# A long-convolution kernel: PSUM banks given out by the scheduler, three filter buffers, and float32r moved from two matmul groups to two others

## The chip, the cores and the metric

The kernel runs on one core of one Trainium2 chip. The metric is the device time of one execution in microseconds (us). Times of a kernel are medians over several executions. Engines are named as in the profile: PE is TensorE (matmuls), PEld its loading of weights, DVE is VectorE, ACT is ScalarE, POOL is GpSimd, SP is the engine that issues transfers. "L710" is line 710 of the kernel. The two versions have different line numbers for the same thing; where it matters, both are given.

## The reference

Four batches of 6272 positions and 256 channels go through a gated recurrence, a projection into three parts, a circular convolution along the positions (by Fourier transform), a product of three, and an output projection.

```python
# x, f_logit: (4, 6272, 256); lower_bound: (256,)
f = lower_bound + (1 - lower_bound) * sigmoid(f_logit)
h = 0
for t in range(6272):                      # the recurrence
    h = f[:, t] * h + (1 - f[:, t]) * x[:, t]
    hh[:, t] = h
x1, x2, x3 = split(hh @ w_proj, 3)         # (4, 6272, 256) each
X2 = rfft(x2, axis=1); H = rfft(filter_fft, axis=0)
y = x1 * irfft(X2 * H, axis=1) * x3
out = y @ w_out                            # float32
```

## The kernel before

The 6272 positions are 49 times 128, and the Fourier transform is made of two matmul stages. For each batch there are three stages that will be called P, U and O.

- **P**: projection to x2 and first transform.
- **U**: sixteen frequency units. Each makes the second transform (TensorE), the product with the filter's transform Hu (VectorE), and the first inverse transform (TensorE).
- **O**: thirteen groups of four residues. Each makes the second inverse transform (TensorE), the product with z = x1 times x3 (VectorE), and the output projection (TensorE).

The recurrence R of the next batch (transposes on TensorE, a scan on VectorE, x1 and x3 on TensorE) has no fixed place; it fills gaps. Before everything comes the preparation, which makes the filter's transform and writes it to DRAM, together with the first R.

No stage is ordered by hand. Every operation is declared with its cost, its reads and its writes. A greedy list scheduler then writes each engine's program: it repeatedly takes the operation that could start first by its estimate and, at equal times, the one with the longest tail behind it. PSUM banks are named in the declaration:

```python
def bank(*k):
    return [("b", i) for i in k]

# U: one pair of banks for the second transform, one for the inverse,
# except in the last batch, which has two of each
k = u % 2
xb, ib = (4 * k, 4 * k + 2) if b == B - 1 else (0, 2)
for i, (p0, p1, q0, ab) in enumerate(((0, TB, 0, 0), (0, Q, Q, 1), (Q, TB, 0, 1))):
    op({"SP": 0.5}, ... dma_start(Hu[p0:p1, k, ab], H[u][q0:q0 + p1 - p0]),
       r=[("H", u)], w=[("Hu", k, i)], kb=2 * (p1 - p0))
op({"PE": 0.5}, mm, r=[("E", u)], w=bank(xb, xb + 1))           # second transform
...
op({"DVE": 1.15}, prod, r=bank(xb + o) + [("Hu", k, i) ...])     # product, L626
...
op({"PE": 0.96}, inv, ..., w=bank(ib, ib + 1))                   # first inverse
```

The output stage writes y in f16 with m outside and the four residues i inside. The projection uses y as its stationary operand and w_out in two f16 halves, Woh + Wol:

```python
y = y[:, :, 0:rn * 128].rearrange("p a (m i) -> p a m i", i=rn)
nc.vector.tensor_tensor(y, PS[...], zr[:, :, :, r0:r0 + rn], op=AOP.mult)       # L672
for i in range(rn):
    for kh in range(2):
        for w in (Woh, Wol):
            nc.tensor.matmul(po[:, i, :], y[:, kh, :, i], w[:, kh, :], ...)     # L685
```

In R, the scan writes h in float32r, x1 and x3 are matmuls from it in float32r (L277), and GpSimd casts h to f16 (L269). In the preparation the filter is rotated by a matmul in plain float32. The copies that wrap h around (`wraps()`) are scheduled only after the preparation has been written out.

Of the kernel before, what the change touches and what calls it, by code (L numbers as in the profile page):

```python
# [21 lines left out]
S = 6272  # L22
# [28 lines left out]
class Plan:  # L51
# [5 lines left out]

    LAT = {"PE": 0.2, "ACT": 0.16, "DVE": 0.14, "POOL": 0.16, "SP": 0.0}
    OWN = {"PE": 0.0, "ACT": 0.1, "DVE": 0.08, "POOL": 0.1, "SP": 0.0}

    def __init__(self):
        self.ops, self.writer, self.readers = [], {}, {}
        self.free = {e: 0.0 for e in self.LAT}
        self.dma = 0.0
        self.table = None

    def op(self, cost, fn, r=(), w=(), kb=0.0, table=None):
# [4 lines left out]
        for t in w:  # L72
            if t in self.writer:
                preds.add(self.writer[t])
            preds.update(self.readers.get(t, ()))
        me = len(self.ops)
        self.ops.append(dict(cost=cost, fn=fn, preds=preds, kb=kb, table=table, end=None,
                             eng=None, succ=[]))
# [16 lines left out]

    def emit(self):
# [8 lines left out]
        while cand:  # L105
            best = None
            for e, f in self.free.items():
                pick = None
                for i in cand:
                    o = ops[i]  # L110
                    if e in o["cost"]:
                        at = max(f, self.ready(o, e))
                        if o["table"] and self.table and o["table"] != self.table:
                            at += 1.3
                        key = (at, -o["level"], i)
                        if pick is None or key < pick:
                            pick = key
                if pick is not None:
                    o = ops[pick[2]]
                    key = (pick[0] + (o["cost"][e] if len(o["cost"]) > 1 else 0.0) * 0.01,  # L120
                           pick[1], pick[2], e, pick[0])
                    if best is None or key < best:
                        best = key
            i, e, at = best[2:]
# [8 lines left out]
            o["fn"](e)  # L133
# [8 lines left out]
def kernel(  # L142
# [29 lines left out]
    W13 = konst.tile([128, 2, 512], F32R, name="W13")  # L172
    W2 = konst.tile([128, 2, 256], F16, name="W2")
    Woh = konst.tile([128, 2, 256], F16, name="Woh")
    Wol = konst.tile([128, 2, 256], F16, name="Wol")
# [10 lines left out]
    hs = konst.tile([128, 2, 2, CH], F32R, name="hs")  # L186
# [3 lines left out]
    H = [dram.tile([TB, 2, UE * 64], F16, name=f"H{u}") for u in range(NU)]  # L190
# [11 lines left out]

    def bank(*k):
        return [("b", i) for i in k]
# [23 lines left out]
    def hgrn(b):  # L228
        z = zt[b % 2]
        for c in range(NCHK):  # L230
# [14 lines left out]
            hk = c % 2  # L245
            for kh in range(2):
                cols = slice(kh * 128, kh * 128 + 128)
                sT, uT = PS[:, 6, 0:n], PS[:, 7, 0:n]

                def turn(e, dst, src, cols=cols, nb=nb):  # L250
                    for j in range(nb):
                        nc.tensor.transpose(dst[:, j * 128:(j + 1) * 128], src[:, j, cols],  # L252
                                            iden[:])
                op({"PE": 0.108 * nb}, lambda e, f=turn, d=sT, s=ft: f(e, d, s),
                   r=[("ft", k)], w=bank(6))
                op({"PE": 0.108 * nb}, lambda e, f=turn, d=uT, s=xt: f(e, d, s),
                   r=[("xt", k)], w=bank(7))
                j = count["f"] % 2
                count["f"] += 1
                fT, h = fTs[:, j, 0:n], hs[:, kh, hk, 0:n]  # L260
                op({"ACT": 0.13 + n / 1200.0}, lambda e, fT=fT, sT=sT, kh=kh:
                   nc.scalar.activation(fT, sT, AF.Identity, scale=nomc[:, kh:kh + 1],  # L262
                                        bias=1.0), r=bank(6), w=[("fT", j)])
                init = 0.0 if c == 0 else hs[:, kh, 1 - hk, CH - 1:CH].bitcast(F32)
                op({"DVE": 0.07 + 2.25 * n / 1000.0}, lambda e, h=h, fT=fT, uT=uT, init=init:
                   nc.vector.tensor_tensor_scan(h, fT, uT, init, op0=AOP.mult, op1=AOP.add),  # L266
                   r=bank(7) + [("fT", j), ("h", kh, 1 - hk)], w=[("h", kh, hk)])
                hn = HA[:, HB[kh] + t0:HB[kh] + t0 + n]
                op({"POOL": 0.1 + n / 1000.0}, lambda e, hn=hn, h=h: nc.gpsimd.tensor_copy(  # L269
                    hn, h.bitcast(F32)), r=[("h", kh, hk)], w=[("hn", kh, c)])  # L270
            for jb in range(2):
                for i in range(2):
                    js = slice(i * 256 + jb * 128, i * 256 + jb * 128 + 128)

                    def mm(e, i=i, js=js, hk=hk, n=n):
                        for kh in range(2):
                            nc.tensor.matmul(PS[:, 4 + i, 0:n], W13[:, kh, js],  # L277
                                             hs[:, kh, hk, 0:n], start=(kh == 0),
                                             stop=(kh == 1))
                    op({"PE": 2 * (0.06 + n / 2400.0)}, mm, r=[("h", 0, hk), ("h", 1, hk)],  # L280
                       w=bank(4 + i))
                j = count["s"] % 2
                count["s"] += 1
                xs = x1s[:, j, 0:n]
                op({"ACT": 0.06 + n / 1200.0}, lambda e, xs=xs, n=n: nc.scalar.activation(  # L285
                    xs, PS[:, 4, 0:n], AF.Copy, scale=ZS), r=bank(4), w=[("x1s", j)])
                op({"DVE": 0.07 + n / 960.0}, lambda e, zz=z[:, jb, t0:t0 + n], xs=xs, n=n:
                   nc.vector.tensor_tensor(zz, PS[:, 5, 0:n], xs, op=AOP.mult),  # L288
                   r=bank(5) + [("x1s", j)], w=[("z", b % 2, jb, c)])
# [12 lines left out]
    def prepare(tmp):  # L302
        dve, pool, act = nc.vector, nc.gpsimd, nc.scalar
        raws = [HA[:, S + 4096 * k:S + 4096 * (k + 1)].bitcast(F32)
                .rearrange("m (r d) -> m r d", d=D) for k in range(3)]
        hws = [HA[:, S + 12288 + 2048 * k:S + 12288 + 2048 * k + 1024]
               .rearrange("p (a n) -> p a n", a=2) for k in range(2)]
# [10 lines left out]
        def oms(e):  # L318
# [6 lines left out]
        wp = raws[0][:, 0:6].rearrange("p a d -> p (a d)").rearrange("p (k j) -> p k j", k=2)  # L325
        wo = raws[1][:, 0:2]
        op({"SP": 0.5}, lambda e: nc.sync.dma_start(
            wp, moe_w_proj.rearrange("(a p) j -> p a j", p=128)), w=E(0, 4096), kb=768)
        op({"SP": 0.5}, lambda e: nc.sync.dma_start(
            wo, moe_w_out.rearrange("(a p) j -> p a j", p=128)), w=E(4096, 8192), kb=256)  # L330
        for kh in range(2):
            small(lambda e, kh=kh: dve.tensor_scalar(
                wp[:, kh, :], in0=wp[:, kh, :], scalar1=omc[:, kh:kh + 1], scalar2=None,
                op0=AOP.mult), 768, r=["om"], w=E(0, 4096))
            for i, j0 in enumerate((0, 512)):
                small(lambda e, kh=kh, i=i, j0=j0: dve.tensor_copy(
                    W13[:, kh, i * 256:(i + 1) * 256], wp[:, kh, j0:j0 + 256]), 256,
                    r=E(0, 4096), w=["W13"])
            for p in range(2):
# [3 lines left out]
                    .rearrange("k (e g) -> k e g", e=2)), 256, r=E(0, 4096), w=["W2"])  # L343
        small(lambda e: dve.tensor_copy(Woh[:], wo[:]), 512, r=E(4096, 8192), w=["Wo"])
        small(lambda e: dve.tensor_tensor(Wol[:], wo[:], Woh[:], op=AOP.subtract), 512,
              r=E(4096, 8192), w=["Wo"])
# [105 lines left out]
        rot = tmp.tile([128, 256], F32, name="rot")  # L452
# [10 lines left out]
        small(gaps, 1920, r=["iden"], w=["f2e"], e="POOL")  # L463
        fv = f2[:, 0:NEP * PW].rearrange("m (g p c) -> m p g c", p=2, c=PW)
        ff = moe_filter_fft.rearrange("(a r) d -> a r d", r=Q)
        for g, r0 in enumerate(range(0, Q, 4)):
            rn = min(4, Q - r0)
            k = (g // 2 + 2) % 3
            raw, et = raws[k], E(4096 * k, 4096 * (k + 1))
# [291 lines left out]
```

## Time and profile before

| | before |
|---|---|
| time, median of 3 runs | 731.81 us (728.07 to 734.73) |
| preparation and first R, with most of a stop at its end | 131 us |
| P of the four batches | 32, 26, 23, 23 us |
| U of the four batches | 70, 76, 76, 54 us |
| O of the four batches | 59, 59, 58, 45 us |
| VectorE's product waiting for Hu | 37.0 us |
| TensorE's second transform waiting for that product | 30.3 us |

Two lines of the profile page of the kernel before give the totals: first the busy time of each engine with its share of the span and its number of instructions, then the clock granted to TensorE in 40 slices of the span, in tenths.

```profile
PE 617.1 (84%) x5262; PEld 471.1 (64%) x5262; DVE 513.9 (70%) x572; ACT 379.6 (52%) x485; POOL 203.2 (28%) x256
...
PEclk9999997699887999999778999999978999955599
```

No engine is busy throughout; in the second U, TensorE and VectorE are each busy for 62 of 76 us. The stage table, the waits and the end of the chain are shown in the prediction below.

### The profile page before, as it was taken

What the parts mean: (1) busy time and instruction counts of PE and PEld (TensorE: products, weight loads), DVE (VectorE), ACT (ScalarE), POOL (GpSimd) and SP (SyncE); (2) the same over time, 40 slices, a digit from 0 to 9 for tenths busy, and PEclk for the clock granted to TensorE, in tenths of its full rate; (3) what the DMA queues carried; (4) which work ended last, traced back from release to release, by engine and by line L of the source; (5) the groups of instructions that cost most, each with busy time, mean ns of one, the idle gap of its engine ahead of it and who ended that gap; (6) DMA issues with size and microseconds to landing.
All of it is one profiled execution on the core that took longest, in us unless ns stands there. A gap on an engine that the chain in (4) does not pass through costs nothing. (4 is left out here: it accounts for less than half of the span.)

```text
span 731.7 us, 13373 instructions
## 1 busy us (share of the span) xinstructions
PE 617.1 (84%) x5262; PEld 471.1 (64%) x5262; DVE 513.9 (70%) x572; ACT 379.6 (52%) x485; POOL 203.2 (28%) x256
## 2 busy tenths in 40 slices
PE   4889993588878999888888999978769999677896
PEld 3767772574546887864556887845448888444585
DVE  8987772389787666697877665898676666967542
ACT  4578882485433555774333556854424547422232
POOL 4335451223323332033223333033324310010000
PEclk9999997699887999999778999999978999955599
DMA  9755646336565757155465766155746732034144
GB/s 308 279 167 162 204 151 232 127 88 204 182 194 175 241 194 268 41 175 175 160 201 181 239 216 239 58 168 181 215 149 227 242 151 82 22 115 131 45 193 160
DMA packets 82161, 126.95 MB, mean 173 GB/s; under 512 B 5454, under 2 KB 56722, under 8 KB 81330
## 3 DMA queue, kind: packets, MB, share of 16 engines
q1 hardware_dynamic: 82098, 126.10, 52.8%
q8 instruction: 41, 0.67, 0.4%
q14 instruction: 22, 0.18, 0.1%
HBM read 84.54 MB, written 28.90 MB: 155 GB/s over the span
## 5 line engine op out<-in xcount | busy, mean ns | idle before, releaser
L626 DVE TENSOR_TENSOR PP<-PS,Hu 98x1008 f16<-98x1008 f32 x128 | 147.8, 1198 | 46.1 <-DMA Hu<-H 37.0
L277 PE MATMUL PS<-hs,W 128*128 128x512 f32 (+1 forms) x416 | 140.5, 432 | 16.3 <-ACT x1s L285 10.9
L243 POOL TENSOR_TENSOR XT<-XT,FL 128x1024 f32<-128x1024 f32 (+1 forms) x52 | 116.7, 2244 | 86.0 <-DMA XT<-in_x_dram 61.2
L209 ACT CAST X<-PS 128x784 f16<-128x784 f32 (+2 forms) x86 | 87.1, 1020 | 86.4 <-PE PS L637 71.7
L269 POOL CAST HA<-hs 128x512 f16<-128x512 f32 (+1 forms) x104 | 61.6, 593 | 245.3 <-DVE hs L266 236.1
L266 DVE TENSOR_TENSOR_SCAN hs<-fTs,hs,PS 128x512 fp32r<-128x512 f32 (+1 forms) x96 | 115.9, 1207 | 10.6 <-PE PS L252 8.9
L672 DVE TENSOR_TENSOR PP<-PS,z 128x1024 f16<-128x1024 f32 (+1 forms) x52 | 61.1, 1184 | 82.7 <-PE PS L663 76.8
L262 ACT ACTIVATE fTs<-PS,nomc 128x512 f32<-128x512 f32 (+1 forms) x104 | 69.1, 665 | 80.1 <-DVE hs L266 42.6
L637 PEld LDWEIGHTS <-PP 98*128 98x128 f16 x1024 | 64.3, 118 | 51.0 <-issue 34.2
L685 PE MATMUL PS<-Woh,PP 128*128 128x256 f16 x392 | 90.3, 278 | 3.4 <-DVE PP L672 3.0
L685 PEld LDWEIGHTS <-PP 128*128 128x128 f16 x784 | 82.6, 114 | 15.8 <-issue 7.6
L277 PEld LDWEIGHTS PS<-hs,W 128*128 128x128 f32 x416 | 66.8, 196 | 35.3 <-ACT x1s L285 15.4
L685 PE MATMUL PS<-Wol,PP 128*128 128x256 f16 x392 | 89.0, 275 | 0.0
L616 PE MATMUL PS<-HA,FT 64*128 64x512 f16 x256 | 59.5, 458 | 31.7 <-DVE PP L626 30.3
L637 PE MATMUL PS<-VA,PP 98*128 98x98 f16 x512 | 72.9, 244 | 15.2 <-DVE PP L626 11.7
L211 ACT ACTIVATE osb<-PS 128x1024 f32<-128x1024 f32 (+1 forms) x51 | 50.3, 986 | 66.3 <-PE PS L685 37.5
L241 ACT ACTIVATE FL<-FL 128x1024 f32<-128x1024 f32 (+1 forms) x52 | 52.4, 1008 | 61.5 <-DMA FL<-in_f_logit_dram 61.5
L288 DVE TENSOR_TENSOR z<-PS,x1s 128x512 f16<-128x512 f32 (+1 forms) x104 | 67.1, 645 | 15.6 <-PE PS L277 9.9
L252 PE MATMUL PS<-iden,FL 128*128 128x128 f32 x392 | 67.1, 295 | 12.8 <-ACT FL L241 10.8
L285 ACT ACTIVATE x1s<-PS 128x512 f32<-128x512 f32 (+1 forms) x104 | 59.3, 570 | 28.9 <-DVE z L288 15.8
L637 PE MATMUL PS<-VB,PP 98*128 98x98 f16 x512 | 73.5, 245 | 0.0
L252 PE MATMUL PS<-iden,XT 128*128 128x128 f32 x392 | 69.9, 304 | 3.4 <-DVE hs L266 3.4
(89 smaller groups left out, 711.3 us busy)
## 6 DMA issues: line engine op xcount, KB each, us to landing
FL<-in_f_logit_dram SPq DMA_DIRECT2D x48, 512.0 KB
XT<-in_x_dram SPq DMA_DIRECT2D x48, 512.0 KB
out_dram<-osb SPq DMA_DIRECT2D x48, 512.0 KB
Hu<-H SPq DMA_DIRECT2D x64, 196.0 KB
Hu<-H SPq DMA_DIRECT2D x128, 98.0 KB
HA<-in_moe_filter_fft_dram SPq DMA_DIRECT2D x6, 1024.0 KB
HA<-HA SPq DMA_DIRECT2D x16, 384.0 KB
H<-HA SPq DMA_DIRECT2D x16, 196.0 KB
```

The costliest lines, as they stand in the source:

```text
L209: nc.scalar.copy(dst, src)
L243: op({"POOL": 0.1 + 0.535 * nb}, lambda e, xt=xt, ft=ft: nc.gpsimd.tensor_tensor(xt, xt, ft, op=AOP.mult), r=[("ft", k)], w=[("xt", k)])
L252: nc.tensor.transpose(dst[:, j * 128:(j + 1) * 128], src[:, j, cols], iden[:])
L262: nc.scalar.activation(fT, sT, AF.Identity, scale=nomc[:, kh:kh + 1], bias=1.0), r=bank(6), w=[("fT", j)])
L266: nc.vector.tensor_tensor_scan(h, fT, uT, init, op0=AOP.mult, op1=AOP.add),
L269: op({"POOL": 0.1 + n / 1000.0}, lambda e, hn=hn, h=h: nc.gpsimd.tensor_copy(hn, h.bitcast(F32)), r=[("h", kh, hk)], w=[("hn", kh, c)])
L277: nc.tensor.matmul(PS[:, 4 + i, 0:n], W13[:, kh, js], hs[:, kh, hk, 0:n], start=(kh == 0), stop=(kh == 1))
L288: nc.vector.tensor_tensor(zz, PS[:, 5, 0:n], xs, op=AOP.mult),
L626: nc.vector.tensor_tensor(PP[:TB, k, o, :, :, 1:64], px.unsqueeze(1).broadcast_to([TB, 2, UE, 63]), hh[:, :, :, 1:64], op=AOP.mult)
L637: nc.tensor.matmul(PS[:, ib + o, pr * TB:(pr + 1) * TB], PP[:TB, k, o, n, 2 * pr:2 * pr + 2, :], v[:TB], start=(n == 0), stop=(n == 1))
L672: nc.vector.tensor_tensor(y, PS[:, cb:cb + 2, 0:rn * 128].rearrange("p a (m i) -> p a m i", i=rn), zr[:, :, :, r0:r0 + rn], op=AOP.mult),
L685: nc.tensor.matmul(po[:, i, :], y[:, kh, :, i], w[:, kh, :], start=(n == 0), stop=(n == 3))
```

## The change

The intent has five parts.

1. **Banks.** An operation says how many banks it takes (`take=2`), the scheduler gives it any free pair, and the readers (`src=`) give it back.
2. **x1 and x3** are computed in f16 from the f16 h, which the scan now writes itself. GpSimd's 104 casts go.
3. **Output projection** in float32r: one matmul instead of two f16 halves, with y and w_out in float32r.
4. **H in three buffers**: the second, swapped copy of each filter tile is written to DRAM once in the preparation, so that a unit needs one load of 392 KB instead of three, and Hu has three buffers instead of two.
5. **Filter rotation** in float32r after a cast, and the wraps in the first schedule.

```diff
+    def room(self, n):
+        best = None
+        for b in range(0, 8, n):
+            if None not in self.bank[b:b + n]:
+                key = (max(self.bank[b:b + n]), n == 1 and self.bank[b ^ 1] is not None, b)
+                if best is None or key < best:
+                    best = key
+        return best
 ...
-    W13 = konst.tile([128, 2, 512], F32R, name="W13")
+    W13 = konst.tile([128, 2, 512], F16, name="W13")
-    Woh = konst.tile([128, 2, 256], F16, name="Woh")
-    Wol = konst.tile([128, 2, 256], F16, name="Wol")
+    Wo = konst.tile([128, 2, 256], F32R, name="Wo")
 ...
-                                             hs[:, kh, hk, 0:n], start=(kh == 0),
+                                             HA[:, HB[kh] + t0:HB[kh] + t0 + n],
 ...
-            pb = 2 * (g % 2)
-            def rotate(e, r0=r0, rn=rn, raw=raw, pb=pb):
+            op({"POOL": 0.1 + 0.3 * rn, "ACT": 0.1 + 0.22 * rn, "DVE": 0.1 + 0.27 * rn},
+               lambda e, raw=raw, fr=fr, rn=rn: copy(e, fr[:, 0:rn], raw[:, 0:rn]),
+               r=et, w=[("af", g % 2)])
+            def rotate(e, pb, r0=r0, rn=rn, fr=fr):
 ...
-            op({"SP": 0.5}, lambda e, hw=hw, u=u: nc.sync.dma_start(H[u][:], hw[:TB]),
-               r=ht, w=[("H", u)], kb=200)
+            for i, (p0, p1, q0) in enumerate(((0, TB, 0), (0, Q, Q), (Q, TB, 0))):
+                op({"SP": 0.5}, lambda e, hw=hw, u=u, p0=p0, p1=p1, q0=q0, ab=min(i, 1):
+                   nc.sync.dma_start(H[u][p0:p1, ab], hw[q0:q0 + p1 - p0]),
+                   r=ht, w=[("H", u, i)], kb=2 * (p1 - p0))
 ...
-            xb, ib = (4 * k, 4 * k + 2) if b == B - 1 else (0, 2)
-            for i, (p0, p1, q0, ab) in enumerate(((0, TB, 0, 0), (0, Q, Q, 1), ...
+            h = (b * NU + u) % 3
+            op({"SP": 0.5}, lambda e, h=h, u=u: nc.sync.dma_start(Hu[:TB, h], H[u][:]),
+               r=[("H", u, i) for i in range(3)], w=[("Hu", h)], kb=400)
 ...
-            op({"PE": 0.5}, mm, r=[("E", u)], w=bank(xb, xb + 1))
+            f2 = op({"PE": 0.5}, mm, r=[("E", u)], take=2)
 ...
-            y = PP[:, yk // 2, yk % 2].rearrange("p a i k -> p a (i k)")
-            y = y[:, :, 0:rn * 128].rearrange("p a (m i) -> p a m i", i=rn)
+            y = ys[:, yk, :, 0:rn * 128].rearrange("p a (m i) -> p a m i", i=rn)
 ...
-                        for w in (Woh, Wol):
-                            nc.tensor.matmul(po[:, i, :], y[:, kh, :, i], w[:, kh, :],
-                                             start=(n == 0), stop=(n == 3))
+                        nc.tensor.matmul(po[:, i, :], y[:, kh, :, i], Wo[:, kh, :],
+                                         start=(kh == 0), stop=(kh == 1))
 ...
-        Hu = cv.tile([128, 2, 2, 2, UE * 64], F16, name="Hu")
+        Hu = cv.tile([128, 3, 2, 2, UE * 64], F16, name="Hu")
+        ys = cv.tile([128, 2, 2, 512], F32R, name="ys")
```

The diff gives y two buffers instead of four.

## The prediction

The sum in it came to 647 us:

- The float32r projection at 125 to 167 ns a matmul (49 to 65 us for 392; in the sum 14 us of the first O, and 1.0 to 1.4 us a group in the last) was an estimate from a rate that no trace shows. A straight line between the two float32r rows that the text names, 112 ns at 128 columns and 231 at 512, gives 152 ns for 256, inside that range; the 0.15 us for a matmul of the rotation, also an estimate, is near it.
- The 24 us of the first P is near the 26, 23 and 23 of the others before.

What the text calls half clock is shown: granted 0.50 from 659 to 687 us, and over the whole kernel before L637 starts every 81 ns where 0.50 was granted and every 43 where it was 1.0.

> **What bounds the kernel now.** I read four views: the page's totals, a table of busy time by stage, the waits, and the chain that ended last. The stages were found by where the groups of TensorE matmuls begin and end in the timeline. A batch has a projection and first transform (P, 23 to 26 us), sixteen frequency units (U) and the output stage (O). The recurrence of the *next* batch (R: transposes, scans, x1 and x3) runs under U and O. Filter preparation and the first R come before all.
>
> The table of stages (length, then busy us and count of PE, PEld, DVE, ACT, POOL, then granted clock, DMA share, GB/s): preparation, then U, O and P of the second batch, then U and O of the last.
> ```profile
> 0.00:131.00 131.00, 100.71 (x597) 77.35 (x597) 91.82 (x164) 84.87 (x119) 53.60 (x76) 0.96 0.67 218
> ...
> 292.00:318.00 26.00, 23.46 (x256) 21.82 (x254) 17.58 (x16) 20.14 (x21) 3.49 (x3) 0.93 0.23 80
> 318.00:394.00 76.00, 62.08 (x472) 40.02 (x471) 62.24 (x61) 33.09 (x46) 24.95 (x33) 0.81 0.56 177
> 394.00:453.00 59.00, 58.60 (x530) 48.04 (x527) 37.01 (x41) 31.16 (x44) 21.01 (x20) 0.98 0.71 237
> ...
> 633.00:687.00 54.00, 39.25 (x324) 22.19 (x323) 39.63 (x36) 13.02 (x17) 5.05 (x16) 0.58 0.35 105
> 687.00:731.70 44.70, 36.73 (x392) 32.72 (x392) 15.37 (x14) 12.67 (x13) 0.00 (x0) 0.92 0.37 145
> ```
> The reader is to see two limits in alternation. O is TensorE's: 58.6 of 59 us. U is VectorE's with holes: 62.2 of 76 us. In U of the last batch nothing else runs, and VectorE is still busy for only 39.6 of 54.
>
> The waits (who waited for whom, us, times, longest):
> ```profile
> DVE PP L626 <- DMA Hu<-H: 37.0, 26, 3.3
> ...
> PE PS L616 <- DVE PP L626: 30.3, 34, 4.1
> ...
> PE PS L550 <- DMA HA<-HA: 17.7, 2, 13.6
> ```
> The first two are the holes of U: VectorE's product waits for the filter tile Hu, and TensorE cannot write the next unit before VectorE has read the single pair of banks. The third is a 13.6 us stop before the first P, because the copies that wrap h around are issued only after the preparation is complete.
>
> The end of the last O, in the chain (start, us, what):
> ```profile
> 694.92 3.62 PE PS L685 x32
> 698.54 1.00 PE PS L663 x16
> 699.54 0.02 issue
> 699.56 1.23 DVE PP L672
> 700.80 0.05 issue
> 700.84 3.68 PE PS L685 x32
> ```
> Two groups take 5.9 us: 32 projection matmuls (3.68), 16 inverse ones, and VectorE in between, exposed.
>
> [...]L685 (256 columns) starts every 109 ns, L565 (128) every 56. [...]weights of L685 take 114 ns, those of float32r L277 take 196. [...]
>
> **The change part by part.**
>
> *Output projection.* Out: 784 f16 matmuls at 109 ns, 85.5 us. In: 392 float32r ones. No row has 128x256 float32r. L277 (512 columns, float32r) starts every 231 ns inside a run[...], and the first of a run costs 85 more (316); L496 (128 columns) every 112. [...] TensorE gets back 20 to 36 us, in O, where it is the bound: 5 to 9 us per batch.
>
> *x1 and x3 in f16.* 416 matmuls in pairs; a pair now takes 316 + 231 = 547 ns, in f16 about 2 x 216 + 60 = 490 or less. That is 12 to 20 us of TensorE, a third in O. GpSimd's 104 casts (61.6 us) go, off the path. The scan stays at 1.27 us.
>
> *Filter rotation.* The old form has 98 rows for 49 products (two passes), each starting 215 ns after the last: 21.1 us. The new: 49 x 0.15 = 7. It adds thirteen casts to float32r, by the order of instructions ten on ScalarE at about 1.0 us and three on GpSimd. TensorE gains 14, ScalarE loses 10. Moreover the wraps are in the first schedule, the filter tiles being laid out clear of them: most of the 17.7 us goes.
>
> *Filter tile.* One load of 392 KB into three buffers instead of three loads into two; the second copy is written once (3.1 MB more). It attacks the 37.0 us, all inside U.
>
> *Banks.* Any free pair instead of fixed ones: attacks the 30.3 us, and the 1.23 us per two groups of the last O.
>
> The order of instructions of the changed kernel shows something the diff does not: in the first U, VectorE has its 32 products without one scan between. All 26 scans of the second batch's R fall into the first O. In the second U there are ten scans, in the third three scans and fourteen x1x3 products.
>
> **Sum by stage**, from what each engine would need:
> - Preparation: VectorE 91.8 + 3 (three more evictions), ScalarE 84.9 + 7, TensorE down to about 80. Plus 10 us of start and some holes: 112 instead of 131.
> - First P: 24 instead of 32[...].
> - First U: 32 products x 1.17 = 37.5 and 1.8 for the edge; TensorE at half clock needs about 2.6 us per unit (1.04 for L616, 2 x 0.62 for L637, and gaps), 42. I take 44, was 70.
> - First O with all of R: TensorE 14 (inverse) + 14 (projection) + 21.4 (196 transposes x 109 ns) + 26 (x1, x3) = 75; VectorE 31.5 (scans) + 17 (x1x3) + 15.4 (products of O) + 4 = 68. Thirteen loads of 1 MB and 6.4 MB of output also want some 250 GB/s. I take 80, was 59.
> - Second and third batch: P 24 and 24 (were 26, 23). U: 37.5 + 1.8 + 13 of scans or x1x3 products = 53, I take 54 each (was 76). O: TensorE about 62 to 68 by the same addition; that addition gives 64 for the old O against 59 measured, so I scale it to 63 and 62 (59, 58).
> - Last: P 23. U 46 (VectorE 41 plus ramp; was 54). O: 13 groups at 2.5 us (TensorE 1.0 + 1.0 to 1.4, output through two buffers) plus ends, 37 (was 45).
>
> 112 + 24 + 44 + 80 + 24 + 54 + 63 + 24 + 54 + 62 + 23 + 46 + 37 = **647 us**, 11.6% less. By stage, U gives 78 us (two waits go, and R moves out), the preparation 19 and P 9; O takes 21 back, because R moves into it, though its own matmuls shrink.
>
> **Rivals.**
> (a) *Loads bound the first O.* x and f_logit keep two buffers, and one chunk's round is load, sigmoid (1.06), GpSimd product (2.37), transposes. At 5.5 to 6.5 us a chunk that is 70 to 85 us, as long as the stage. For it: loads already stop ScalarE for 61.5 us. If copies queue, this O takes 90 to 95 and the total is 660. Against: only 0.71 of the DMA engines' time was used at 237 GB/s.
> (b) *The clock takes it back.* [...]TensorE at half clock (42 us) bounds U. With transposes on top, U of the middle batches is 60: total 660.
> (c) *Projection in float32r is not cheaper*, its weights being loaded with a stride[...]. At 218 ns it gives back 9 us per batch: total about 675.
> (d) *The schedule fits better than I think.* VectorE needs about 515 us in all; at 85% busy (70% now) the time is 606.
>
> **Range.** Taking out two measured waits (67 us, near the bound in U) and 46 to 70 us of TensorE gives a clear gain; (a) to (c) together hardly undo it. I predict 647, 8 in 10 between 618 and 682. Faster by over 2%: 0.97; within 2%: 0.02; slower: 0.01.
>
> **What would show it.** Right: waits of L658 (the product) for Hu under 8 us in all; waits of L648 for it under 10; first P starting near 112 us with no multi-microsecond stop on a copy; the first and last U 42 to 46 us with VectorE over 85% busy; the float32r projection starting every 125 to 167 ns; GpSimd near 140 us busy; total VectorE unchanged near 515. Wrong: a first O over 90 us with waits on x or f_logit (rival a); U of the middle batches at 60 or more with a clock under 0.75 (b); the projection at 200 ns or more (c). The whole would be wrong if evictions to other types, or scans writing f16, were slower than their old rows.

## More of the kernel before

The granted clock is lowest in the last U (slices of 5 tenths; 0.50 from 659 to 687 us). It falls to 7 in the other U stages, and to 7 and 6 around a stop before the first P. The border of 131 us lies inside that stop: TensorE began P at 116.9 us, ran three matmuls of it, and stood from 121.9 to 135.5 us until the wrapped h was there.

## The result, and the profile after

| | before | after |
|---|---|---|
| time, median of 4 runs each | 729.94 us (725.3 to 734.73) | 655.06 us (654.2 to 659.61) |
| span of the profiled execution | 731.7 us | 653.4 us |
| mean granted clock of it | 0.899 | 0.953 |

The ratio is 0.8986 with a 95% interval from 0.8911 to 0.9062. A ratio here is the mean time of one kernel's fast runs over that of the other's of the same rounds, so it is not quite the ratio of the medians quoted. The prediction was 647 us with a range from 618 to 682: the measured 655.06 is inside and 8 us above its centre.

The totals and the clock of the page of the changed kernel:

```profile
PE 559.9 (86%) x4821; PEld 430.0 (66%) x4821; DVE 512.2 (78%) x576; ACT 381.2 (58%) x490; POOL 149.8 (23%) x161
...
PEclk9989999899979999998898999999899999997898
```

VectorE has the same work as before (512.2 against 513.9 us) in a shorter span. TensorE has 57 us less. The slices at 5 tenths of the clock are gone.

The table by stage of the changed kernel (stretch, its length, then busy us and instructions of PE, PEld, DVE, ACT, POOL, then granted clock, DMA share, GB/s). The rows are the preparation; P, U and O of the first batch; U and O of the second; U and O of the last:

```profile
0.00:122.60 122.60, 92.36 (x546) 63.53 (x547) 92.07 (x168) 86.96 (x120) 40.34 (x51) 0.93 0.70 238
122.60:145.60 23.00, 18.85 (x226) 18.11 (x226) 17.47 (x15) 20.68 (x20) 6.31 (x4) 1.00 0.64 185
145.60:186.10 40.50, 29.29 (x344) 18.18 (x344) 40.35 (x38) 16.08 (x20) 7.15 (x17) 0.95 0.60 179
186.10:266.70 80.60, 78.85 (x578) 62.97 (x579) 62.35 (x66) 46.97 (x70) 24.70 (x13) 0.98 0.78 264
...
292.00:351.00 59.00, 43.45 (x420) 30.40 (x418) 51.73 (x48) 25.84 (x34) 16.43 (x21) 0.86 0.71 210
351.00:407.60 56.60, 55.60 (x420) 45.44 (x420) 36.58 (x39) 30.97 (x44) 14.94 (x7) 1.00 0.77 264
...
567.70:610.30 42.60, 33.85 (x349) 19.44 (x348) 40.49 (x40) 16.14 (x22) 5.05 (x16) 0.84 0.41 124
610.30:653.40 43.10, 37.35 (x295) 33.05 (x294) 16.36 (x16) 12.95 (x15) 0.00 (x0) 0.96 0.37 150
```

In U of the first batch VectorE is now busy for 40.35 of 40.5 us: the holes are closed. The first O has become the longest stage, with TensorE busy for 78.85 of 80.6 us, because the whole R of the second batch moved into it. All thirteen stages, in us:

| | prep. | P | U | O | P | U | O | P | U | O | P | U | O |
|---|---|---|---|---|---|---|---|---|---|---|---|---|---|
| before | 131 | 32 | 70 | 59 | 26 | 76 | 59 | 23 | 76 | 58 | 23 | 54 | 45 |
| predicted | 112 | 24 | 44 | 80 | 24 | 54 | 63 | 24 | 54 | 62 | 23 | 46 | 37 |
| after | 122.6 | 23.0 | 40.5 | 80.6 | 25.3 | 59.0 | 56.6 | 24.5 | 48.9 | 66.0 | 20.7 | 42.6 | 43.1 |

The waits of the changed kernel (who waited for whom, us in all, times, longest), those that answer to the three shown before:

```profile
PE PS L648 <- ACT X L246: 19.2, 19, 3.1
...
PE PS L589 <- DMA HA<-HA: 1.6, 1, 1.6
DVE PP L658 <- DMA Hu<-H: 1.5, 2, 1.0
...
PE PS L648 <- DVE PP L658: 0.9, 2, 0.7
```

The product (L658, before L626) waited 37.0 us for Hu and now waits 1.5. The second transform (L648, before L616) waited 30.3 us for the product and now waits 0.9. The first projection waited 17.7 us for the wrapped h and now waits 1.6. What remains for L648 is 19.2 us on ScalarE's copy out of PSUM.

The end of the last O of the changed kernel in the chain of waits (start, us, what):

```profile
622.55 2.08 PE PS L710 x8
624.63 0.98 PE PS L693 x16
625.61 2.07 PE PS L710 x8
627.68 0.98 PE PS L693 x16
```

A group now takes 2.07 + 0.98 = 3.05 us, all of it TensorE's. VectorE's product is no longer in the chain. But the eight matmuls of the projection take 2.07 us. Before, 32 matmuls for two groups took 3.68 us, which is 1.84 us for one group. The projection has got *slower*. The groups of the changed kernel show where (busy us, mean ns of one, idle before):

```profile
L710 PE MATMUL PS<-Wo,ys 128*128 128x256 f32 x392 | 102.5, 405 | 0.5 <-DVE ys L700 0.5
L710 PEld LDWEIGHTS PS<-Wo,ys 128*128 128x128 f32 x392 | 94.1, 325 | 5.6 <-issue 3.7
```

The weight loads of the kernel before, for comparison:

```profile
L685 PEld LDWEIGHTS <-PP 128*128 128x128 f16 x784 | 82.6, 114 | 15.8 <-issue 7.6 <-DVE PP L672 7.2
```

One weight load takes 325 ns on average, and TensorE spends 94.1 us on them, where 784 f16 loads took 82.6. The matmuls are listed as 405 ns long, more than the distance between their starts, and their ends are modelled, so that mean is no rate. What counts is the distance from one start to the next, read from the start times in the trace: a median of 234 ns for L710 against 109 ns for each of the two f16 matmuls that it replaces.

### The profile page after: what moved, and what is told of

Read it like the earlier page. It is cut to its first block, busy times and chain, and to the rows that moved or that the text cites. A ratio compares the mean times of both kernels' runs of the same rounds, so it can differ in the third digit from the quotient of the medians.

```text
span 653.4 us, 12392 instructions
## 1 busy us (share of the span) xinstructions
PE 559.9 (86%) x4821; PEld 430.0 (66%) x4821; DVE 512.2 (78%) x576; ACT 381.2 (58%) x490; POOL 149.8 (23%) x161
## 4 chain that ended last, share of the span: by engine, by line
PE 53%; DVE 14%; DMA 13%; ACT 7%; issue 5%; POOL 2%; SPq 1%; DVEq 0%; ACTq 0%; POOLq 0%
PE PS L710 13%; PE PS L287 10%; PE PS L315 8%; DVE PP L658 8%; PE PS L693 6%; DMA FL<-in_f_logit_dram 6%; PE PS L589 5%; PE PS L668 3%; PE PS L604 2%; PE PS L648 2%; DVE HA L304 2%; ACT X L246 2%; DMA XT<-in_x_dram 2%; DMA H<-HA 2%; DMA Hu<-H 2%
## 5 line engine op out<-in xcount | busy, mean ns | idle before, releaser
L658 DVE TENSOR_TENSOR PP<-PS,Hu 98x1008 f16<-98x1008 f32 x128 | 145.6, 1200 | 8.9 <-PE PS L648 3.0
L304 DVE TENSOR_TENSOR_SCAN HA<-fTs,HA,PS 128x512 f16<-128x512 f32 (+1 forms) x96 | 114.6, 1205 | 29.2 <-PE PS L287 20.7
L315 PE MATMUL PS<-HA,W 128*128 128x512 f16 (+1 forms) x416 | 106.5, 376 | 6.0 <-DVE HA L304 3.9
L710 PE MATMUL PS<-Wo,ys 128*128 128x256 f32 x392 | 102.5, 405 | 0.5 <-DVE ys L700 0.5
L710 PEld LDWEIGHTS PS<-Wo,ys 128*128 128x128 f32 x392 | 94.1, 325 | 5.6 <-issue 3.7
L700 DVE TENSOR_TENSOR ys<-PS,z 128x1024 fp32r<-128x1024 f32 (+1 forms) x52 | 60.6, 1178 | 42.0 <-PE PS L693 37.6
L668 PE MATMUL PS<-VA,PP 98*128 98x98 f16 x512 | 62.7, 220 | 21.7 <-DVE PP L658 9.9
L287 PEld LDWEIGHTS PS<-iden,XT 128*128 128x128 f32 x392 | 48.1, 148 | 25.2 <-POOL XT L280 10.4
L315 PEld LDWEIGHTS <-W 128*128 128x128 f16 x416 | 37.4, 100 | 39.3 <-issue 15.3
L287 PEld LDWEIGHTS PS<-iden,FL 128*128 128x128 f32 x392 | 49.3, 152 | 19.6 <-ACT FL L278 9.8
L648 PE MATMUL PS<-HA,FT 64*128 64x512 f16 x256 | 41.8, 402 | 20.8 <-ACT X L246 19.2
L693 PE MATMUL PS<-ID,X 64*128 64x128 f16 x784 | 51.3, 309 | 1.0 <-ACT X L248 0.5
```

The costliest lines, as they stand in the source:

```text
L287: nc.tensor.transpose(PS[:, p, j * 128:(j + 1) * 128], src[:, j, cols], iden[:])
L304: nc.vector.tensor_tensor_scan(h, fT, PS[:, p, 0:n], init, op0=AOP.mult, op1=AOP.add),
L315: nc.tensor.matmul(PS[:, p, 0:n], W13[:, kh, js], HA[:, HB[kh] + t0:HB[kh] + t0 + n], start=(kh == 0), stop=(kh == 1))
L658: nc.vector.tensor_tensor(PP[:TB, k, o, :, :, 1:64], px.unsqueeze(1).broadcast_to([TB, 2, UE, 63]), hh[:, :, :, 1:64], op=AOP.mult)
L668: nc.tensor.matmul(PS[:, ib + o, pr * TB:(pr + 1) * TB], PP[:TB, k, o, n, 2 * pr:2 * pr + 2, :], v[:TB], start=(n == 0), stop=(n == 1))
L693: nc.tensor.matmul(PS[:, cb + p, i:i + rn * 127 + 1:rn], tf[ps, c0:c0 + 128], ID[ps, rr, sh:sh + 128], start=(rr == 0), stop=(rr == 1))
```

## The experiments

Twelve kernels ran, in three calls. Each was timed in three rounds (four executions) beside the kernel before on the same chip (seven executions, medians of 729.16, 729.65 and 730.26 us). All intervals are 95%. Edits are against the changed kernel. It ran again in the first call only, so in the other two calls a difference to it in us is one between two chips; the ratios to the kernel before are taken on one chip each.

### The changed kernel again

No edit.

> The changed kernel itself, as the base of this chip for the other three. Both theories: ratio to before 0.89 to 0.91, projection matmul L710 starting every 233 ns inside a run, first P at about 123 us.

Measured: 655.87 us, ratio 0.8998 [0.8933, 0.9062]. The first P began at 119.8 us, the second U took 59.2 us, the last O 43.2 us, and L710 started every 234 ns. The result repeats.

### Why the float32r projection starts every 234 ns: y laid out in rows

The weights of L710 are y[:, kh, :, i], every fourth element of a row: a step of 8 bytes when y was f16, of 16 bytes now. This edit lays each residue's 128 values side by side, so that the weights are contiguous. VectorE then writes them with a step.

```diff
-            y = ys[:, yk, :, 0:rn * 128].rearrange("p a (m i) -> p a m i", i=rn)
+            y = ys[:, yk, :, 0:rn * 128].rearrange("p a (i m) -> p a m i", i=rn)
```

> Only the layout of y in its tile changes: the 128 columns that a projection matmul loads as weights lie side by side instead of 16 bytes apart. The order of instructions stays the same. Theory S (the step of the float32r weights makes the load slow): L710 starts every 114 to 125 ns, its weight load takes about 190 ns instead of 329, TensorE gets back about 98 x 110 ns = 10.8 us per batch, the last O falls from 43 us to 31 to 37, the whole to 618 to 635 us (ratio to before 0.845 to 0.87). Theory F (float32r[...] costs this for 256 columns, whatever the layout): L710 stays at 233 ns, the ratio at 0.90. A side effect to watch is VectorE's product L700, which now writes with a step: 1.18 us now.

Measured: 637.26 us, ratio 0.8724 [0.8669, 0.878], correct. L710 now starts every 120 ns, and the last O takes 34.5 us. The groups of this experiment, each shape apart:

```profile
L700 DVE TENSOR_TENSOR ys<-PS,z 128x1024 fp32r<-128x1024 f32 x48 | 93.8, 1983 | 8.0 <-PE PS L693 6.6 <-ACT osb L248 0.7
...
L710 PE MATMUL PS<-Wo,ys 128*128 128x256 f32 x392 | 59.2, 294 | 8.6 <-DVE ys L700 8.1
...
L710 PEld LDWEIGHTS PS<-Wo,ys 128*128 128x128 f32 x392 | 49.8, 189 | 18.6 <-DVE ys L700 10.7 <-issue 5.1 <-ACT FL L278 2.3
```

The same row of the product in the repeated changed kernel reads:

```profile
L700 DVE TENSOR_TENSOR ys<-PS,z 128x1024 fp32r<-128x1024 f32 x48 | 57.7, 1216 | 39.1 <-PE PS L693 34.6 <-ACT osb L248 4.4
```

The weight load falls from 325 to 189 ns. So float32r alone does not cost the 234 ns: without the step it starts every 120. Nor does a step alone. The projection to x2 (L589) takes its weights from the f16 h with a step of 49 elements, 98 bytes. In the repeated changed kernel:

```profile
L589 PEld LDWEIGHTS <-HA 128*128 128x128 f16 x392 | 43.1, 142 | 3.9 <-DMA HA<-HA 1.8 <-issue 1.6
```

These loads take 142 ns, where contiguous f16 ones take 98 (L604, L315), and the matmul, also of 256 columns, still starts every 109 ns. It is the two together, four-byte weights and a step of 16 bytes, that cost the 234 ns; float32r with a step of 8 bytes was not run. TensorE gets 392 x (234 - 120) = 45 us back. But VectorE's product rises from 1216 to 1983 ns, 48 x 767 ns = 37 us more. The two lie on different engines, and the sum on the clock is a gain of 19 us. Moving the step from one reader to one writer has not removed it.

### Is it any step in the write, or the pitch of 512 bytes? Rows 528 bytes apart

```diff
-            y = ys[:, yk, :, 0:rn * 128].rearrange("p a (m i) -> p a m i", i=rn)
+            y = ys[:, yk, :, 0:rn, 0:128].rearrange("p a i m -> p a m i")
...
-        ys = cv.tile([128, 2, 2, 512], F32R, name="ys")
+        ys = cv.tile([128, 2, 2, 4, 132], F32R, name="ys")
```

> As e1 (columns of y side by side, same order of instructions), but the rows of y lie 528 bytes apart instead of 512. In e1 L710 came to 120 ns, but VectorE's product L700 rose from 1216 to 1983 ns for 1024 elements. Theory A (a write step of 512 bytes is the bad one): L700 returns to 1.2 to 1.3 us, L710 stays at 120 ns, the whole 618 to 632 us (ratio 0.845 to 0.867). Theory B (any write that steps costs it): L700 about 2.0 us, the time as in e1 (ratio 0.87).

Measured: 633.38 us, ratio 0.8675 [0.8621, 0.8728], correct. L710 starts every 118 ns. The product of this experiment:

```profile
L700 DVE TENSOR_TENSOR ys<-PS,z 128x1024 fp32r<-128x1024 f32 x48 | 92.7, 1967 | 9.3 <-PE PS L693 8.5 <-ACT osb L248 0.7
```

1967 against 1983 ns: with this pitch the step in the write costs the same. Other pitches were not run. The intervals of the two runs overlap.

### The step put into the read of z instead

Here the inverse transform writes PSUM one residue after another, y is written without a step, and VectorE reads z (f16) with a step of 98 bytes.

```diff
-                            nc.tensor.matmul(PS[:, cb + p, i:i + rn * 127 + 1:rn],
+                            nc.tensor.matmul(PS[:, cb + p, i * 128:(i + 1) * 128],
...
-            y = ys[:, yk, :, 0:rn * 128].rearrange("p a (m i) -> p a m i", i=rn)
+            y = ys[:, yk, :, 0:rn * 128].rearrange("p a (i m) -> p a i m", i=rn)
...
-                   zr[:, :, :, r0:r0 + rn], op=AOP.mult),
+                   zr[:, :, :, r0:r0 + rn].rearrange("p a m i -> p a i m"), op=AOP.mult),
```

> As e1, but the step is moved from the write to the read: the inverse matmuls write the four rows of a group one after the other in PSUM, VectorE writes y without a step and reads the f16 gate z with a step of 98 bytes. Same order of instructions. If only stepped writes are slow: L700 1.2 us, L710 120 ns, 618 to 632 us (ratio 0.845 to 0.867). If a stepped f16 read is as slow: L700 near 2 us, ratio 0.87 as in e1.

Measured: 651.96 us, ratio 0.8919 [0.8862, 0.8976], correct. L710 starts every 120 ns, but the product is the dearest of all three forms:

```profile
L700 DVE TENSOR_TENSOR ys<-PS,z 128x1024 fp32r<-128x1024 f32 x48 | 112.4, 2382 | 4.0 <-PE PS L693 3.8
...
L693 PE MATMUL PS<-ID,X 64*128 64x128 f16 x784 | 32.7, 224 | 3.9 <-DVE ys L700 1.1 <-DVE osb L253 0.8 <-ACT X L248 0.5
```

It gives nearly everything back: VectorE is busy for 565.3 us of this run, and the time is about that of the changed kernel. One thing came along unasked. The inverse matmuls L693, whose results are no longer written to PSUM with a step, were busy for 32.7 us here and for 51.3 in the changed kernel, with the same count of 784.

### The projection in two f16 halves, as before

```diff
-    Wo = konst.tile([128, 2, 256], F32R, name="Wo")
+    Woh = konst.tile([128, 2, 256], F16, name="Woh")
+    Wol = konst.tile([128, 2, 256], F16, name="Wol")
...
-                        nc.tensor.matmul(po[:, i, :], y[:, kh, :, i], Wo[:, kh, :],
-                                         start=(kh == 0), stop=(kh == 1))
+                        for w in (Woh, Wol):
+                            nc.tensor.matmul(po[:, i, :], y[:, kh, :, i], w[:, kh, :],
+                                             start=(n == 0), stop=(n == 3))
+                            n += 1
...
-        ys = cv.tile([128, 2, 2, 512], F32R, name="ys")
+        ys = cv.tile([128, 2, 2, 512], F16, name="ys")
```

> The projection of the kernel before (y and two f16 halves of the weights, 16 matmuls per group of four) in the changed kernel. My reading of the trace: 16 x 109 ns = 1.74 us per group against 8 x 233 = 1.87, so the time is the same as that of the changed kernel within 1% or up to 1% less (ratio 0.89 to 0.905). If float32r did save what I predicted (8 x 125 to 167 ns), this would be 20 us slower or more (ratio 0.925 or higher).

Measured: 651.27 us, ratio 0.8927 [0.8857, 0.8998], correct; starts every 109 ns, last O 40.7 us. Undoing this part of the change does not cost time: the median is 4.6 us lower, with overlapping intervals. By the start-to-start times it should save 392 x (234 - 2 x 109) = 6 us. As built, the float32r projection is worth nothing or slightly less.

### Banks fixed again

`room()` may give only two pairs to transforms and projections, and four single banks to R.

```diff
-        for b in range(0, 8, n):
+        for b in ((0, 2) if n == 2 else (4, 5, 6, 7)):
```

> The scheduler may use only bank pairs 0-1 and 2-3 for two-bank results and banks 4 to 7 for single ones, about as the kernel before did for all but its last batch (the order of instructions follows from it and changes too). Theory B (free banks removed the 30.3 us of waits of the frequency matmul for the product, and the exposed product in the last O): waits of L648 for L658 come back to 10 to 35 us, the last U goes from 42 us to 50 or more, the last O from 43 to 48 or more, the whole to 675 to 715 us (ratio 0.925 to 0.98). Rival (the banks were not the limit, the order of the work was): under 665 us (ratio below 0.91).

Measured: 722.48 us, ratio 0.9905 [0.9826, 0.9984], correct. Nearly the whole gain goes. P took 38.8, 35.5, 35.8 and 35.4 us, and U 62.0, 59.4, 62.9 and 56.4. The waits of this run:

```profile
PE PS L648 <- ACT X L246: 45.7, 38, 3.5
...
PE PS L648 <- DVE PP L658: 2.0, 3, 0.7
```

The wait does not come back in its old form (on the product, only 2.0 us). It comes back on ScalarE's copy of the inverse, 45.7 us instead of 19.2, which fits that the two pairs are now shared by the second transform and the inverse. The edit is harsher than the kernel before, which used four pairs in P and three in the first transform: P took 145.5 us in all, against 104 in the kernel before and 93.5 in the changed one, and U 240.7 against 276 and 191 (O was 37 us shorter than in the changed kernel). So the 67 us are not the share of the free banks, and are likely above it. The order was planned anew as well, so banks and order are not taken apart here.

### Two buffers for Hu instead of three, in the same order

```diff
-            h = (b * NU + u) % 3
+            h, hb = (b * NU + u) % 3, (b * NU + u) % 2
...
-        Hu = cv.tile([128, 3, 2, 2, UE * 64], F16, name="Hu")
+        Hu = cv.tile([128, 2, 2, 2, UE * 64], F16, name="Hu")
```

> The filter tile Hu in two buffers instead of three, the order of instructions kept. Theory 3 (the third buffer removed VectorE's 37.0 us of waits for Hu): waits of L658 for Hu come back to 15 to 35 us, the total rises by 10 to 25 us (ratio 0.91 to 0.935). Theory 1 (the single load of all 98 rows in place of three loads did it): waits for Hu under 8 us, ratio 0.90 to 0.905.

Measured: 808.46 us, ratio 1.1062, and a **wrong result** (relative error 1.166). This experiment was badly built. The order planned for three buffers puts a later load ahead of earlier products, and with two buffers in memory that load goes into the buffer that those products still want (the product waited 152.4 us for such loads). It tells nothing of the question, and its time is not used.

### Two buffers for Hu, with the scheduler knowing

```diff
-            h = (b * NU + u) % 3
+            h = (b * NU + u) % 2
...
-        Hu = cv.tile([128, 3, 2, 2, UE * 64], F16, name="Hu")
+        Hu = cv.tile([128, 2, 2, 2, UE * 64], F16, name="Hu")
```

> The filter tile in two buffers, this time known to the scheduler, since keeping the order with fewer buffers gave a wrong result and an order that makes products wait for later loads (152 us of waits). Theory 3 (the third buffer matters): waits of L658 for Hu of 12 us or more, ratio 0.91 to 0.935. Theory 1 (the single load did it): waits for Hu under 8 us and the time within 1.5% of the changed kernel (ratio 0.887 to 0.913); the order of instructions differs, so a few us are not to be read.

Measured: 671.42 us, ratio 0.9203 [0.9135, 0.9271], again with a **wrong result** (relative error 0.061). In the order of this build, twelve of the thirteen groups of the last batch's projection (96 matmuls from 550.9 us on) run, and are copied to X2, before the last four inverse matmuls of the third batch's O (562.4 us). X2 and Th share memory, and the declarations say nothing between them, which fits the error but was not proved to be its cause. No instruction is left out, so the time is used with that caution. The waits of this run:

```profile
DVE PP L658 <- DMA Hu<-H: 18.2, 16, 3.9
```

The wait on Hu comes back with 18.2 us, about half of the old 37.0, and the time rises by about 15 us. So the third buffer removes about 17 us of the wait (18.2 against 1.5). That the single load of 392 KB removed the rest is likely but not shown, since the banks and the order differ from the kernel before too.

### The same, with x1 and x3 in float32r

To the edit before this adds the old form of R: `hs` in float32r, the cast on GpSimd, and W13 in float32r.

```diff
-    W13 = konst.tile([128, 2, 512], F16, name="W13")
+    W13 = konst.tile([128, 2, 512], F32R, name="W13")
+    hs = konst.tile([128, 2, 2, CH], F32R, name="hs")
...
-                h = HA[:, t1:t1 + n]
+                h = hs[:, kh, hk, 0:n]
...
-                                             HA[:, HB[kh] + t0:HB[kh] + t0 + n],
+                                             hs[:, kh, hk, 0:n],
```

> e4 with x1 and x3 again in float32r from a separate h and GpSimd's 104 casts back (two filter buffers, because h takes their space). To be compared with e4. My step: a pair of x1/x3 matmuls falls from 547 ns to about 440 to 490, 12 to 22 us of TensorE in all, a good half of it on the path: e5 is 8 to 20 us slower than e4 (ratio higher by 0.011 to 0.028). Rival (hidden beside VectorE, which needs 515 us in both): under 5 us.

Measured: 681.95 us, ratio 0.9309 [0.9234, 0.9383], correct. Against the run before it that is 0.0106 of the kernel before, about 8 us by the ratios and 10 by the medians. The two intervals overlap, the order was planned anew, and the run that it is compared with gave a wrong result, so this is the expected direction and no firm size. x1 and x3 in f16 start every 216 ns, in float32r every 231, and 314 where the pair begins.

### Four buffers for H in the preparation

The preparation stood out, 10.6 us longer than predicted. In its chain of waits in the changed kernel (start, us, what), stores of finished filter tiles to DRAM appear between the evictions:

```profile
84.97 4.12 DMA H<-HA
89.20 1.03 ACT HA L248
90.96 3.86 DMA H<-HA
95.03 1.22 DVE HA L253
...
107.35 4.34 DMA H<-HA
111.81 1.24 DVE HA L253
```

The next tile can only be copied out of PSUM when one of the two buffers has been stored, some 4 us. This edit gives four.

```diff
-               for a in (6144, 8192)]
+               for a in (6144, 7168, 8192, 9216)]
...
-            hw = hws[u % 2]
-            ht = E(6144 + 2048 * (u % 2), 6144 + 2048 * (u % 2) + 2048)
+            hw = hws[u % 4]
+            ht = E(6144 + 1024 * (u % 4), 6144 + 1024 * (u % 4) + 1024)
```

> The filter's output tile in the preparation gets four buffers in the same space instead of two. Theory H (in the second half of the preparation VectorE and ScalarE wait for the store of the tile to land: 12 us on the chain that ended last): the first P starts at 113 to 117 us instead of 122.6 and the whole is 5 to 9 us shorter. Rival V (VectorE with 92 of 122.6 us and ScalarE with 87 are the limit and the store only fills their pauses): the first P moves by less than 2 us.

Measured: 685.95 us, ratio 0.9402 [0.9345, 0.9459], correct, and neither theory had it. The filter was finished at 101.7 us instead of 118.7, but the first P began at 149.2 us instead of 119.8. Freed from the buffers, the greedy scheduler ran the filter ahead of everything and left the recurrence, which the first P needs, for the end. A freer resource made the schedule 30 us worse.

### Four buffers in memory, the order unchanged

The same memory, but the declarations still speak of two buffers, so that the order on each engine is that of the changed kernel.

```diff
-               for a in (6144, 8192)]
+               for a in (6144, 7168, 8192, 9216)]
...
-            hw = hws[u % 2]
+            hw = hws[u % 4]
```

> The four buffers of e7 in the kernel alone; the scheduler still believes in two, so every engine has exactly the order of the changed kernel. In e7 the scheduler used the freedom to finish the filter 17 us earlier and left the recurrence for the end: 30 us slower. Theory H (the store's landing, 12 us on the chain, limits the second half of the preparation): with the order kept, first P at 113 to 118 us instead of 120 to 123, total 3 to 8 us less (ratio 0.888 to 0.896). Theory V (VectorE and ScalarE limit it): under 2 us, ratio 0.897 to 0.90.

Measured: 650.39 us, ratio 0.8906 [0.8856, 0.8956], correct. In the repeated changed kernel these waits stood:

```profile
ACT HA L248 <- DMA H<-HA: 4.9, 6, 1.7
...
DVE HA L253 <- DMA H<-HA: 4.2, 5, 1.3
```

In this run there is no wait on that store at all. The first P began at 117.4 us (119.8 and 122.6 in the changed kernel). So the stores account for some 2 to 5 us of the preparation; with overlapping intervals of the totals it is a direction, not a firm number.

### The combination: one f16 matmul in the projection, and the four buffers

In f16 the projection started every 109 ns with its step of 8 bytes (the kernel before, and two f16 halves again), although a weight load took 114 ns there against 98 without a step; in float32r with 16 bytes it started every 234. So by these runs y in f16 needs no other layout. With w_out in one f16 tile instead of two halves there is also one matmul instead of two. The order is that of the changed kernel.

```diff
-    Wo = konst.tile([128, 2, 256], F32R, name="Wo")
+    Wo = konst.tile([128, 2, 256], F16, name="Wo")
...
-            hw = hws[u % 2]
+            hw = hws[u % 4]
...
-        ys = cv.tile([128, 2, 2, 512], F32R, name="ys")
+        ys = cv.tile([128, 2, 2, 512], F16, name="ys")
```

> What e1, e9 and e10 point to: the contiguous weights of e1 need a stepped write, which VectorE pays for (1967 to 2382 ns instead of 1217). In f16 the 8-byte step costs the weight load nothing (109 ns start to start in e2). So y and the output weights in f16, one matmul instead of two halves, plus the four buffers of e7b; the order of instructions is that of the changed kernel. Expected: 8 x 109 = 0.87 us a group instead of 1.87, L700 at 1.22 us, last O 30 to 33 us, total 610 to 624 us (ratio 0.835 to 0.856). If the time given back is lost to another wait (loads, out buffers): 630 us or more. The precision falls by the rounding of the output weights to f16; it is to be seen whether the result passes.

Measured: **615.16 us**, ratio 0.8415 [0.8352, 0.8479], correct by the comparison with the reference (w_out and y are rounded to f16 here, which costs accuracy that was not measured apart). The projection in this run:

```profile
L710 PE MATMUL PS<-Wo,ys 128*128 128x256 f16 x392 | 50.7, 274 | 0.8 <-DVE ys L700 0.4
```

It starts every 109 ns. TensorE needs 392 x (234 - 109) = 49 us less, and 41 us of that and of the four buffers together arrive in the time. The last O takes 32.2 us instead of 43.1. It is the fastest version here, 16% under the kernel before and 6% under the changed one.

## Why the prediction was right or wrong

**The mechanism was right for U and the wraps.** The two waits of U were named as the holes, and they closed: 37.0 to 1.5 us and 30.3 to 0.9. U of all batches went from 276 to 191 us (predicted 198). The wait on the wraps fell from 17.7 to 1.6 us. The prediction called U VectorE's, although both engines were busy for 62 us of the 76; the first U bears it out (VectorE 40.35, TensorE 29.29 of 40.5 us), the second less (51.73 and 43.45 of 59).

The move of R into the first O, read from the order of instructions, came as forecast. That its length matched, 80.6 us against 80, is partly luck: from start to start the projection took 23.8 us there where the sum has 14, x1 and x3 took 21.7 where it has 26, and transposes and inverse 20.7 and 12.6 (21.4 and 14), so that the 5 us taken on top of the sum of 75 were used up by the projection. VectorE's total stayed (512.2 against the 515 stated), and so did the costs that might have undone the whole: a scan, now to f16, took 1205 ns on average (1207 before), the product of O, now to float32r, 1178 (1184). The experiments weigh the parts: fixing the banks takes away 67 us, going back to two buffers about 15, x1 and x3 in float32r some 8 to 10, none of them the exact share of its part. These do not add up, since the scheduler makes a new order each time.

**The step that failed is the size of the float32r projection.** It was put at 125 to 167 ns a matmul, a gain of 20 to 36 us of TensorE. Measured: 234 ns, 392 x 234 = 92 us against 85.5 before, a loss of 6 us. Rival (c) had it, with its 218 ns and weights "loaded with a stride", but was weighed too lightly. The stride is what the first edit took away, and with contiguous weights the same matmul starts every 120 ns. The rotation (L519), also float32r and contiguous, started every 113 to 124 ns inside a run in the trace of the changed kernel, where a clock of 1.0 was granted (213 to 219 where it was 0.50). The estimate was therefore right for a contiguous operand and wrong for this one, whose step doubled in bytes when its type did.

The weight loads side by side, mean ns of one: in f16 98 without a step (L604 and L315 in the repeated changed kernel), 114 with one of 8 bytes (L685 in the kernel before) and 142 with one of 98 bytes (L589 in the repeated changed kernel); in float32r L710 189 without a step (the first edit) and 325 with one of 16 bytes (the changed kernel). The f16 loads with a step took 16 and 44 ns more, the float32r one 136. On VectorE's side, the product took 1216 ns when it wrote float32r without hops, 1983 with hops of 512 bytes (1.63 times), and 2382 when it read z, in f16, with a step of 98 bytes instead. Why a step costs what it does was not shown.

**Why the total was still close.** Errors of both signs cancelled, which is luck. Too low were the preparation (+10.6 us), the last O (+6.1), the second U (+5.0) and the third O (+4.0). The last O is the projection's: 13 groups at the predicted 2.5 us, measured 3.05, are 7 us. The third O was not taken apart. In the second U, 45% of the chain that ended last are loads (f_logit 22.3%, Hu 11.7%, x 11.0%); no experiment tested them. Too high were U of the first, third and last batch (-3.5, -5.1, -3.4), the second O (-6.4) and the last P (-2.3). All thirteen differences sum to 653.4 - 647 = 6.4 us.

**The preparation** was predicted from VectorE's sum with 17 us of start and holes (112 - 94.8). VectorE's busy time was 92.07, near the 94.8 estimated, but start and holes were 122.6 - 92.07 = 30.5 us. Waiting for the stores to DRAM is part of it (2 to 5 us by the four-buffer run). The rest was not taken apart and stays open. Moreover the old 131 us held some 14 us that were no preparation but the stop on the wraps. TensorE began P at 116.9 us in the kernel before and at 122.6 (119.8 in the repeat) in the changed one, so the preparation itself became 3 to 6 us longer, though TensorE's busy time in it fell from 100.7 to 92.4 us. What was gained by the end of the first P, 163.0 to 145.6 us, is about the 17.7 us of the stop.

**The rivals.** (a) Loads as the bound of the first O: refuted, TensorE was busy for 78.85 of 80.6 us. (b) A clock that takes the gain back: refuted for the mean, which rose from 0.899 to 0.953; the second U did take 59.0 us, near the 60 named, but at a clock of 0.86, with VectorE busy for 51.7. TensorE's busy share did not tell the clock here: the last U before had TensorE busy for 73% at a clock of 0.58, with no pause over 1.86 us, and the first U after for 72% at 0.95. (c) is near in its number (218 against 234) and right in naming the stride, but its total of 675 us was not reached. (d) A schedule that fits better: partly, in U. VectorE was busy for 78%, not 85; the combined experiment, with its 615 us at 83%, came near it.

The rotation and the wraps were not tried apart. By the times above, the stop on the wraps is enough for the 8 us by which the border of the preparation moved; no gain from the rotation is to be seen in them.

## What to carry to other kernels

When an operand changes from two bytes to four, recompute its step in bytes for every engine that reads or writes it, before trusting a duration from another row of the same type (here 109 ns at 8 bytes in f16, 234 at 16 bytes in float32r, 120 in float32r without a step); and if a step only moves from one engine to another, ask which of the two is the bound in that stage. With a greedy scheduler, test a buffer twice, once with the order kept and once with the plan made anew: the first tells what the buffer is worth (here about 5 us, with overlapping intervals), the second what the new order does (here 30 us to the worse). And keep the order only where every instruction's dependences still hold in the smaller memory, or the run tells nothing.

One layout between the two was not run: y in pairs, two residues side by side, so that VectorE writes runs of two words and TensorE reads with a step of 8 bytes. What either engine takes then is not shown by any run here.
